# The end of a mixer kernel: last tile in three pieces, stores from ScalarE, no block around the program

## The chip, the cores and the metric

The kernel runs on one core of a Trainium2 chip. The time is the device time of one execution in microseconds (us), given as the median of several runs. Beside it stands a profiled execution, whose span runs from the first to the last instruction in the trace; an execution's time is somewhat longer than its span.

The engines of a core are TensorE (PE: matmuls; PEld: its weight loads), VectorE (DVE), ScalarE (ACT), GpSimd (POOL) and SyncE (SP, which here does nothing but issue transfers). Each runs its own list of instructions, and they wait for each other through semaphores. A transfer (DMA) is issued by an engine, moved by 16 DMA engines, and raises a semaphore when it has landed.

## The reference

```python
def reference(x, w1, w2, w3, w4):          # x: 1 x 2048 x 512, bf16
    B, S, D = x.shape
    h = _gelu(_layernorm(x, axis=-1) @ w1)             # w1: 512 x 512
    c = D // 4
    g0 = jnp.pad(h[:, :, 0*c:1*c], ((0, 0), (1, 0), (0, 0)))[:, :S, :]
    g1 = jnp.pad(h[:, :, 1*c:2*c], ((0, 0), (0, 1), (0, 0)))[:, 1:, :]
    g2 = jnp.pad(h[:, :, 2*c:3*c], ((0, 0), (2, 0), (0, 0)))[:, :S, :]
    g3 = jnp.pad(h[:, :, 3*c:   ], ((0, 0), (0, 2), (0, 0)))[:, 2:, :]
    hs = jnp.concatenate([g0, g1, g2, g3], axis=-1) @ w2   # w2: 512 x 512
    x1 = x + hs
    h2 = _gelu(_layernorm(x1, axis=-1) @ w3) @ w4      # w3: 512 x 1792, w4: 1792 x 512
    return x1 + h2
```

For the change only the last line matters: each output row is x1 plus a product with w4 that sums over 1792 = 14 x 128 hidden values.

## The kernel before

The 2048 rows are 16 tiles of 128. Each tile passes through a layer norm, a transpose, the product with w1 and a gelu ("up1"), the product with w2 on rows shifted by one or two ("mix"), a second layer norm and transpose, the product with w3 and a gelu ("up2"), and the product with w4 ("down"). A list, `SCRIPT`, gives the order of these steps for TensorE. A planner (`Program.order`) goes through all operations, with estimated durations and due times, and writes down one order per engine. `emit` then walks the plan and writes each operation into its engine's program, ahead of it the waits on semaphores that it needs (L635).

The names that the change touches:

- `mm_down` makes the down step of one tile: 14 matmuls (L511) into one bank of `o_ps`, a PSUM tensor with two banks that are used in turn; then a residual addition on VectorE (L519) from PSUM and x1 into `o_sb`; then a store of `o_sb` to the output (L522), issued by SP. A matmul that reuses a bank waits for the addition that last read it.
- `TAIL` gives the column pieces of the last tile (`last`, tile 15). All other tiles are done in one piece of 512 columns. With (256, 256) the last tile has two chains of 14 matmuls, two additions of 256 columns and two stores of 64 KB, each with rows of 512 bytes.
- `emit` opens a block (`with nc.Block() as block:`, L593). Each engine's instructions stand in a body of that block, which the engine branches into at the start. At the end of the block each engine drains, and a barrier over all five engines is passed: GpSimd gathers their arrivals and releases them. These instructions carry L593.
- After all operations SP waits for the semaphores of all 17 stores in turn (L655).

The last steps of TensorE are down 10, down 14 and down 15. ScalarE's last work is the gelu of the last up2 group, which is done about 101 us into the run. ScalarE issues one transfer in the whole kernel: half of the first tile of x (L292), whose other half SP issues.

Of the kernel before, what the change touches and what calls it, by code (L numbers as in the profile page):

```python
# [12 lines left out]
ENGINES = ["sp", "act", "pe", "dve", "pool"]  # L13
# [178 lines left out]
SQRT = (0,)  # L192
STAT_ACT = (1, 3, 6, 16, 23)
HALF = (0,)
TAIL = (256, 256)
LOADS = """
x2 x1 x0 x4-5 w1b w1a x3 w2 x6-7 w3 x8-11 x12-15 w4b tp19 w4a
"""
# [6 lines left out]
def bass_standalone__mixer_s_mlp__prompt_kernel(nc, x, w1, w2, w3, w4, out):  # L205
    B, S, D = x.shape
# [13 lines left out]
    with ExitStack() as es:  # L220
# [31 lines left out]
        pg = Program()  # L252
# [6 lines left out]
        def next_bank():  # L259
            nbank[0] += 1  # L260
            return (nbank[0] - 1) % NOB, nbank[0]
# [236 lines left out]
        def mm_down(t):  # L498
            g = group_of[2, t]
            oi = t % NO  # L500
            last = t == NT - 1
            c0 = 0
            for hh, W in enumerate(TAIL if last else (D,)):
                b, v = next_bank()
                dst = o_ps[:, b, 0:W]
                cs = slice(c0, c0 + W)
                c0 += W

                def f(e, dst=dst, cs=cs):
                    for fc in range(FC):  # L510
                        ins = e.matmul(dst, h2T[:, fc, P * t : P * (t + 1)], w4_sb[:, fc, cs],  # L511
                                       start=(fc == 0), stop=(fc == FC - 1))
                    return ins

                pg.add("pe", f"down{t}_{hh}", f,
                       reads=[(("w4", c), 0) for c in range(FC)] + [(("h2", j, g), 0) for j in range(FC)],
                       writes=[(("o", b), v)], dur=FC * (W * 0.4167 + 2.5))
                pg.add("dve", f"res{t}_{hh}",
                       (lambda d, c: (lambda e: e.tensor_tensor(o_sb[:, oi, c], d, x1_sb[:, t, c], ALU.add)))(dst, cs),  # L519
                       reads=[(("o", b), v), (("x1", t), 0)], writes=[(("osb", oi, hh), t)], dur=70 + W * 1.04)  # L520
                pg.add("sp", f"out_dma{t}_{hh}",
                       (lambda c: (lambda e: e.dma_start(outt[:, t, c], o_sb[:, oi, c])))(cs),  # L522
                       reads=[(("osb", oi, hh), t)], dur=400 * W / D, queue="sp")


        consts()
# [15 lines left out]
        if SQRT:  # L542
            pg.add("act", "warm_sqrt", lambda e: e.activation(warm[:], eps_c[:], ACT_F.Sqrt),
                   reads=[(("eps",), 0)], writes=[(("warm",), 0)], dur=1400)
        pg.add("act", "warm_gelu", lambda e: e.activation(warm[:], eps_c[:], ACT_F.Gelu_apprx_tanh),
               reads=[(("eps",), 0)] + [(("sdv", q), 0) for q in SQRT], writes=[(("warm",), 1)], dur=1400)
        steps = []
        for step in SCRIPT.split():
            kind, n = step.split(":")
            a, _, b = n.partition("-")  # L550
            steps += [(kind, n) for n in (range(int(a), int(b or a) + 1) if kind != "warm" else [int(n)])]
        pe_tp = {n for kind, n in steps if kind in ("tp", "ty")}
        queue = []
# [11 lines left out]
        for kind, n in steps:  # L565
            if kind == "warm":
                warm_pe(n)
            elif kind in ("tp", "ty"):
                pe_transpose(n % NT, n, kind == "ty")
            elif kind == "mix":  # L570
                mm_mix(n)
            elif kind == "down":
                mm_down(n)
            else:
                for _ in mm_up(int(kind[2]), n):
                    pass
        pg.line(queue)
        pg.order()
        emit(nc, es, pg)

def emit(nc, es, prog):

    engs = {"sp": nc.sync, "act": nc.scalar, "pe": nc.tensor, "dve": nc.vector, "pool": nc.gpsimd}
    sems = {e: es.enter_context(nc.semaphore("sem_" + e)) for e in ENGINES}
    ndma = 0
    for op in prog.seq:
        if op.queue is not None:
            op.stream = ("dma", ndma)
            sems[op.stream] = es.enter_context(nc.semaphore(f"sem_dma{ndma}"))
            ndma += 1  # L590
        else:
            op.stream = op.eng
    with nc.Block() as block:  # L593
        bodies = {}

        def keep(name):
            def _body(e):
                bodies[name] = nc.cur_body

            return _body  # L600

        block.gpsimd(keep("pool"))
        block.sync(keep("sp"))
        block.scalar(keep("act"))
        block.vector(keep("dve"))
        block.tensor(keep("pe"))
        know = {e: {} for e in ENGINES}
        implied = {}
        count = {}
        last_write, readers = {}, {}  # L610
        for op in prog.seq:
            e = op.eng
            needs = {}

            def need(sv):
                if needs.get(sv[0], 0) < sv[1]:
                    needs[sv[0]] = sv[1]

            for res, ver in op.reads:
                lw = last_write[res]  # L620
                assert lw[2] == ver, (op.name, res, ver, lw)
                need(lw)
            for res, ver in op.writes:
                if res in last_write:
                    need(last_write[res])
                for sv in readers.get(res, ()):
                    need(sv)
            if e == "pe":
                needs.pop("pe", None)
            k = know[e]  # L630
            with nc.body(bodies[e]):
                for s, v in sorted(needs.items(), key=lambda sv: -sv[1]):
                    if k.get(s, 0) >= v:
                        continue
                    engs[e].wait_ge(sems[s], v)  # L635
                    for s2, v2 in implied[(s, v)].items():
                        if v2 > k.get(s2, 0):
                            k[s2] = v2
                    k[s] = max(k.get(s, 0), v)
                ins = op.fn(engs[e])  # L640
                inc = 1 if op.queue is None else 16
                ins.then_inc(sems[op.stream], inc)
            val = count[op.stream] = count.get(op.stream, 0) + inc
            snap = dict(k)
            snap[op.stream] = max(snap.get(op.stream, 0), val)
            implied[(op.stream, val)] = snap
            for res, ver in op.reads:
                readers.setdefault(res, []).append((op.stream, val))
            for res, ver in op.writes:
                last_write[res] = (op.stream, val, ver)  # L650
                readers[res] = []
        with nc.body(bodies["sp"]):
            for op in prog.seq:
                if op.name.startswith("out_dma"):
                    nc.sync.wait_ge(sems[op.stream], 16)  # L655


# [26 lines left out]
```

## Time and profile before

| | us |
|---|---|
| median of 12 runs | 138.71 (138.18 to 139.49) |
| the profiled execution's time | 138.38 |
| its span | 136.6 |
| TensorE busy | 131.7 (96%) |
| VectorE, ScalarE, GpSimd busy | 58.8, 51.4, 19.4 |
| granted TensorE clock | 1.00 |

How to read it: a line of the profile names a group of instructions by the line of the kernel, the engine, the operation and the tiles written and read (out<-in), with counts, total and mean durations. "SPq" and "ACTq" are the sequencers of those engines, where transfers are issued. The chain of waits follows the work that ended last back to what released it; "issue" is time in which an engine waited for nothing that the profile shows. The timeline gives start and length in us from the start of the span; in brackets stands the idle time before an instruction and what ended it.

### The profile page before, as it was taken

The page shows a single profiled execution, that of the slowest core. Times are in us where ns is not written, and L with a number is a line of the kernel's source. Part 1 is how long each engine was busy: PE and PEld are TensorE (multiplying, and loading weights), DVE is VectorE, ACT ScalarE, POOL GpSimd, SP SyncE. Part 2 cuts the span into 40 slices and gives each one's busy share as a digit, 9 for nine tenths or more (in the row PEclk, how much of TensorE's full clock was granted, in tenths as well). Part 3 has the DMA queues.
Part 4 walks back from the last instruction along what each step waited for, and adds up shares of the span by engine and source line. Part 5 has one row for each costly group of instructions (what it writes and reads, how often), then busy time and mean ns, then how long its engine had stood idle before and what let it go on. Part 6 is the DMA issues. An engine that isn't in the chain of part 4 may idle for free.

```text
span 136.6 us, 1976 instructions
## 1 busy us (share of the span) xinstructions
PE 131.7 (96%) x773; PEld 73.3 (54%) x786; DVE 58.8 (43%) x169; ACT 51.4 (38%) x70; POOL 19.4 (14%) x43
## 2 busy tenths in 40 slices
PE   6989999999999999999999999999999999999992
PEld 2277878776668644444444444444444444444471
DVE  1797999998899640043610053210002222322231
ACT  4799657443667455530055520025550000000000
POOL 2342383332043410001010010000000000000000
DMA  4899966474269551001210003110001111111111
GB/s 107 288 347 403 364 224 118 94 100 79 59 211 187 100 103 38 0 0 38 82 38 0 0 0 76 40 38 5 0 0 34 43 38 38 43 38 38 51 64 41
DMA packets 21257, 12.19 MB, mean 89 GB/s; under 512 B 13568, under 2 KB 20736, under 8 KB 21248
## 3 DMA queue, kind: packets, MB, share of 16 engines
q1 hardware_dynamic: 21104, 12.00, 33.0%
q8 instruction: 6, 0.10, 0.3%
q10 hardware_dynamic: 144, 0.07, 0.2%
q14 instruction: 3, 0.02, 0.1%
HBM read 6.82 MB, written 2.10 MB: 65 GB/s over the span
## 4 chain that ended last, share of the span: by engine, by line
PE 85%; DVE 5%; POOL 3%; DMA 2%; issue 1%; SPq 1%; ACT 0%
PE y_ps L442 40%; PE o_ps L511 35%; PE o_ps L482 9%; POOL rstd L366 3%; DMA x_sb<-in_x_dram 2%; DVE xn_buf L372 1%; DVE st L349 1%; PE y_ps L415 1%; DVE x_sb L493 1%; POOL xn_buf L383 1%; SPq L296 1%; DVE x_sb L489 1%; DVE st6b L343 0%; DVE o_sb L519 0%; DVE vpe L355 0%
## 5 line engine op out<-in xcount | busy, mean ns | idle before, releaser
L442 PE MATMUL y_ps<-xnT,w_sb 128*128 128x256 bf16 (+2 forms) x435 | 64.1, 305 | 0.3
L442 PEld LDWEIGHTS y_ps<-xnT,w_sb 128*128 128x128 bf16 x440 | 40.4, 98 | 23.7 <-issue 0.2
L511 PE MATMUL o_ps<-w_sb,h2T 128*128 128x512 bf16 (+1 forms) x236 | 48.8, 366 | 0.1
L457 ACT ACTIVATE h2T<-y_ps 128x1024 bf16<-128x1024 f32 (+1 forms) x29 | 28.6, 994 | 36.6 <-PE y_ps L442 36.5
L511 PEld LDWEIGHTS o_ps<-w_sb,h2T 128*128 128x128 bf16 x238 | 23.3, 98 | 25.3
L519 DVE TENSOR_TENSOR o_sb<-o_ps,x_sb 128x512 bf16<-128x512 f32 (+1 forms) x17 | 11.2, 660 | 44.6 <-PE o_ps L511 44.3
L366 POOL TENSOR_TENSOR rstd<-vpe,neghalf 128x1 f32<-128x1 f32 x31 | 16.9, 558 | 61.8 <-DVE vpe L355 53.4
L493 DVE TENSOR_TENSOR x_sb<-o_ps,x_sb 128x512 bf16<-128x512 f32 x14 | 9.6, 689 | 22.2 <-PE o_ps L482 22.2
L349 DVE BATCH_NORM_STATS2 st<-x_sb 128x6 f32<-128x512 bf16 x26 | 17.5, 684 | 2.2 <-DMA x_sb<-in_x_dram 2.1
L482 PE MATMUL o_ps<-w_sb,hT 128*128 128x512 bf16 x58 | 15.0, 379 | 0.3
L372 DVE TENSOR_SCALAR xn_buf<-x_sb,mv,rstd 128x512 bf16<-128x512 bf16 x25 | 10.2, 411 | 3.8 <-POOL rstd L366 2.8
L457 ACT ACTIVATE hT<-y_ps 128x1024 bf16<-128x1024 f32 (+1 forms) x10 | 8.5, 852 | 7.7 <-PE y_ps L442 7.6
L482 PEld LDWEIGHTS o_ps<-w_sb,hT 128*128 128x128 bf16 x64 | 6.1, 98 | 5.3
L535 PE MATMUL o_ps<-zeros 128*128 128x512 bf16 x12 | 5.2, 627 | 1.2 <-DVE zeros L269 1.2
L380 ACT ACTIVATE xn_buf<-x_sb,nmr,rstd 128x512 bf16<-128x512 bf16 x5 | 4.0, 810 | 2.6 <-DVE nmr L376 2.6
L351 DVE BATCH_NORM_AGGREGATE mv<-st 128x2 f32<-128x6 f32 x26 | 4.1, 173 | 0.2
L535 PEld LDWEIGHTS o_ps<-zeros 128*128 128x128 bf16 x12 | 1.7, 145 | 3.9 <-issue 2.7
L355 DVE TENSOR_SCALAR vpe<-mv 128x1 f32<-128x1 f32 x26 | 3.5, 148 | 0.3
L324 ACT ACTIVATE junk<-x_sb 128x512 bf16<-128x512 bf16 x5 | 3.1, 628 | 0.7 <-DVE x_sb L489 0.7
L415 PEld LDWEIGHTS y_ps<-ident,xn_buf 128*128 128x128 bf16 x28 | 1.8, 98 | 1.8 <-DVE xn_buf L372 1.3
L415 PE MATMUL y_ps<-ident,xn_buf 128*128 128x128 bf16 x28 | 2.4, 220 | 0.3 <-DVE xn_buf L372 0.2
L420 ACT ACTIVATE xnT<-y_ps 128x512 bf16<-128x512 bf16 (+1 forms) x5 | 2.6, 548 | 0.1
(33 smaller groups left out, 18.9 us busy)
## 6 DMA issues: line engine op xcount, KB each, us to landing
out_dram<-o_sb SPq DMA_DIRECT2D x15, 128.0 KB, 1.7
w_sb<-in_w_dram SPq DMA_DIRECT2D x1, 1792.0 KB, 10.0
w_sb<-in_w_dram SPq DMA_DIRECT2D x2, 896.0 KB, 9.6
x_sb<-in_x_dram SPq DMA_DIRECT2D x2, 512.0 KB, 12.0
x_sb<-in_x_dram SPq DMA_DIRECT2D x2, 256.0 KB, 4.7
w_sb<-in_w_dram SPq DMA_DIRECT2D x2, 256.0 KB, 3.7
w_sb<-in_w_dram SPq DMA_DIRECT2D x1, 512.0 KB, 5.8
x_sb<-in_x_dram SPq DMA_DIRECT2D x3, 128.0 KB, 2.4
```

The source lines that it names most:

```text
L349: pg.add("dve", f"bnst{q}", lambda e: e.bn_stats(st6[:, q, :], src), reads=rs, writes=[(("st6", q), 0)], dur=605)
L351: pg.add("dve", f"bnag{q}", lambda e: e.bn_aggr(mv[:, q, :], st6[:, q, :]), reads=[(("st6", q), 0)], writes=[(("mv", q), 0)], dur=75)
L366: lambda e: e.tensor_tensor(col(rstd), col(vpe), neghalf[:], ALU.pow),
L372: lambda e: e.tensor_scalar(dst, src, mv[:, q, 0:1], rstd[:, q : q + 1], ALU.subtract, ALU.mult),
L415: ins = e.transpose(chunk(c), xn_buf[:, slot(q), P * c : P * (c + 1)], ident[:])
L442: ins = e.matmul(y_ps[:, p, W * i : W * (i + 1)], wsb[:, dc, P * fc : P * (fc + 1)], src[:, dc, P * t0 : P * t0 + W], start=(dc == 0), sto ...
L457: (lambda d, s: (lambda e: e.activation(d, s, ACT_F.Gelu_apprx_tanh)))(dst, ysrc),
L482: ins = e.matmul(dst, hT[:, j, c0 : c0 + P], w2_sb[:, j, :], start=(j == 0), stop=(j == DC - 1))
L493: f = lambda e: e.tensor_tensor(x1_sb[:, t, :], dst, x_sb[:, t, :], ALU.add)
L511: ins = e.matmul(dst, h2T[:, fc, P * t : P * (t + 1)], w4_sb[:, fc, cs], start=(fc == 0), stop=(fc == FC - 1))
L519: (lambda d, c: (lambda e: e.tensor_tensor(o_sb[:, oi, c], d, x1_sb[:, t, c], ALU.add)))(dst, cs),
L535: ins = e.matmul(o_ps[:, b, :], zeros[:, 0:P], zeros[:], start=True, stop=True)
```

## The change

The last tile is made in three pieces of 256, 128 and 128 columns. Its three stores are issued by ScalarE and no longer by SP; the last two are of 32 KB, with rows of 256 bytes. `emit` writes all instructions straight into the program, with no block: the branch into the block, the branch out of it, the drains and the closing barrier are gone. SP still waits for all stores (now 18) at the end. The plan of everything else is the same: on every engine the other instructions stand in the same order with the same waits.

```diff
-TAIL = (256, 256)
+TAIL = (256, 128, 128)
...
-                pg.add("sp", f"out_dma{t}_{hh}",
+                pg.add("act" if last else "sp", f"out_dma{t}_{hh}",
                        (lambda c: (lambda e: e.dma_start(outt[:, t, c], o_sb[:, oi, c])))(cs),
-                       reads=[(("osb", oi, hh), t)], dur=400 * W / D, queue="sp")
+                       reads=[(("osb", oi, hh), t)], dur=400 * W / D, queue="act" if last else "sp")
...
-    with nc.Block() as block:
-        bodies = {}
-
-        def keep(name):
-            def _body(e):
-                bodies[name] = nc.cur_body
-
-            return _body
-
-        block.gpsimd(keep("pool"))
-        block.sync(keep("sp"))
-        block.scalar(keep("act"))
-        block.vector(keep("dve"))
-        block.tensor(keep("pe"))
...
-            with nc.body(bodies[e]):
-                for s, v in sorted(needs.items(), key=lambda sv: -sv[1]):
...
-                ins = op.fn(engs[e])
-                inc = 1 if op.queue is None else 16
-                ins.then_inc(sems[op.stream], inc)
+        for s, v in sorted(needs.items(), key=lambda sv: -sv[1]):
...
+        ins = op.fn(engs[e])
+        inc = 1 if op.queue is None else 16
+        ins.then_inc(sems[op.stream], inc)
...
-        with nc.body(bodies["sp"]):
-            for op in prog.seq:
-                if op.name.startswith("out_dma"):
-                    nc.sync.wait_ge(sems[op.stream], 16)
+    for op in prog.seq:
+        if op.name.startswith("out_dma"):
+            nc.sync.wait_ge(sems[op.stream], 16)
```

The rest of the diff is the same code with one level of indentation less.

More of the change, by code (lines that the diff above doesn't have):

```diff
@@ L592, in emit @@
             op.stream = op.eng
-    with nc.Block() as block:
-        bodies = {}
-        def keep(name):
-            def _body(e):
-                bodies[name] = nc.cur_body
-            return _body
-        block.gpsimd(keep("pool"))
-        block.sync(keep("sp"))
-        block.scalar(keep("act"))
-        block.vector(keep("dve"))
-        block.tensor(keep("pe"))
[L607 to L610, printed above, removed]
-        for op in prog.seq:
[L612 to L630, printed above, removed]
-            with nc.body(bodies[e]):
-                for s, v in sorted(needs.items(), key=lambda sv: -sv[1]):
[L633 to L639, printed above, removed]
-                ins = op.fn(engs[e])
-                inc = 1 if op.queue is None else 16
-                ins.then_inc(sems[op.stream], inc)
[L643 to L651, printed above, removed]
-        with nc.body(bodies["sp"]):
-            for op in prog.seq:
-                if op.name.startswith("out_dma"):
-                    nc.sync.wait_ge(sems[op.stream], 16)
@@ new lines, in emit, with need @@
+    know = {e: {} for e in ENGINES}
+    implied = {}
+    count = {}
+    last_write, readers = {}, {}
+    for op in prog.seq:
+        e = op.eng
+        needs = {}
+        def need(sv):
+            if needs.get(sv[0], 0) < sv[1]:
+                needs[sv[0]] = sv[1]
+        for res, ver in op.reads:
+            lw = last_write[res]
+            assert lw[2] == ver, (op.name, res, ver, lw)
+            need(lw)
+        for res, ver in op.writes:
+            if res in last_write:
+                need(last_write[res])
+            for sv in readers.get(res, ()):
+                need(sv)
+        if e == "pe":
+            needs.pop("pe", None)
+        k = know[e]
+        for s, v in sorted(needs.items(), key=lambda sv: -sv[1]):
+            if k.get(s, 0) >= v:
+                continue
+            engs[e].wait_ge(sems[s], v)
+            for s2, v2 in implied[(s, v)].items():
+                if v2 > k.get(s2, 0):
+                    k[s2] = v2
+            k[s] = max(k.get(s, 0), v)
+        ins = op.fn(engs[e])
+        inc = 1 if op.queue is None else 16
+        ins.then_inc(sems[op.stream], inc)
+        val = count[op.stream] = count.get(op.stream, 0) + inc
+        snap = dict(k)
+        snap[op.stream] = max(snap.get(op.stream, 0), val)
+        implied[(op.stream, val)] = snap
+        for res, ver in op.reads:
+            readers.setdefault(res, []).append((op.stream, val))
+        for res, ver in op.writes:
+            last_write[res] = (op.stream, val, ver)
+            readers[res] = []
@@ L659 @@
+    for op in prog.seq:
+        if op.name.startswith("out_dma"):
+            nc.sync.wait_ge(sems[op.stream], 16)
 _INS = ['x', 'w1', 'w2', 'w3', 'w4']
```

## The prediction, made before the result was known

> **What bounds the kernel now.** I read the page's busy times first, then the chain of waits at the two ends of the run, then the timeline of the last microseconds, and last the DMA table and the records of the closing barrier.
>
> The busy line shows which engine sets the pace:
>
> ```profile
> PE 131.7 (96%) x773; PEld 73.3 (54%) x786; DVE 58.8 (43%) x169; ACT 51.4 (38%) x70; POOL 19.4 (14%) x43
> ```
>
> TensorE is busy for 96% of the 136.6 us span, and the other engines for less than half of it. The chain of waits, from 100 us on, says that nothing but matmuls stands on the path until the last one is done:
>
> ```profile
> 99.99 0.81 PE y_ps L442 x3
> 100.80 9.93 PE o_ps L511 x46
> ...
> 121.58 12.52 PE o_ps L511 x71
> 134.09 0.02 issue
> 134.11 0.42 DVE o_sb L519
> ```
>
> So the time is made of a head (before TensorE has work), a body that this change doesn't touch, and a tail of 136.6 - 134.1 = 2.5 us after the last matmul. The change touches one branch in the head, the last 1.5 us of matmuls, and the tail. The timeline of the tail (start, length):
>
> ```profile
> 131.11 0.69 DVE L519 TENSOR_TENSOR o_sb<-o_ps,x_sb 128x512 bf16<-128x512 f32 x1 [2.39 <-PE o_ps L511]
> 132.59 0.42 DVE L519 TENSOR_TENSOR o_sb<-o_ps,x_sb 128x256 bf16<-128x256 f32 x1 [0.78 <-PE o_ps L511]
> 134.11 0.42 DVE L519 TENSOR_TENSOR o_sb<-o_ps,x_sb 128x256 bf16<-128x256 f32 x1 [1.10 <-PE o_ps L511]
> ...
> 134.57 0.33 SPq L522 DMA_DIRECT2D out_dram<-o_sb  x1
> ```
>
> The second residual addition ends at 134.11 + 0.42 = 134.53; SP issues the last store at 134.57. The records of SP's final waits (L655) and of the closing block (L593), asked for the stretches in which they fall, give the rest:
>
> ```profile
> L655 SPq EVENT_SEMAPHORE  x1: 28/28/28, 136.1 to 136.1; - x1
> L593 SPq COMPARE_BRANCH  x1: 33/33/33, 136.2 to 136.2; - x1
> L593 SPq DRAIN  x1: 7/7/7, 136.3 to 136.3; - x1
> L593 POOLq EVENT_SEMAPHORE  x2: 17/17/17, 136.4 to 136.5; - x2
> L593 PEldq EVENT_SEMAPHORE  x1: 51/51/51, 136.5 to 136.5; - x1
> ```
>
> The last wait starts in the stretch 136.10 to 136.15, so it is done by about 136.15. Then SP branches, drains, tells GpSimd, which gathers and releases all five engines; TensorE's release ends the span at 136.6. The tail is therefore 0.44 residual addition and hop, 1.54 from the store's issue to its landing, about 0.03 wait record, and 0.45 closing barrier.
>
> **The change part by part.**
>
> *The closing barrier goes.* In the changed kernel SP's last instruction is the last of its waits for the stores. Removed: branch, drain, gather, release, 136.15 to 136.6. All of it stood on the path, since nothing runs beside it: -0.45 us. Bounds: -0.40 (the records' rounding) to what lies outside the span. The profiled execution took 138.38 us with a span of 136.6, so 1.78 us are not in the span. If the four other engines now end their own programs up to 30 us before SP does, some of that 1.78 may leave the path too; I take nothing for it and keep a case for it. The Trainium skill (Runtime: NRT & Kernel Launch, "The ~15µs preamble/postamble breakdown") says that the runtime puts its own barrier of about 1.5 us behind a kernel to wait for all engines. By that rule the kernel's barrier is a second one, and its removal loses no order; it could speak against the change only if the runtime's barrier grew by what ours shrank, and then the sum would be without the 0.45. The trace ends before it. I take the row, because SP, the last to arrive, arrives 0.45 earlier.
>
> *The branch at the start goes.* The chain of waits has 0.07 us of issue ahead of SP's first load, against 0.06 and 0.05 ahead of the next ones:
>
> ```profile
> 0.65 0.07 issue
> 0.72 0.40 SPq L296
> 1.12 0.06 issue
> 1.18 0.42 SPq L296
> 1.60 0.05 issue
> ```
>
> A branch costs between 0 and 0.07 here; the one branch with a record took 33 ns. I take -0.03. The first loads stand on the chain, so the whole run moves by it.
>
> *The last tile in three pieces.* In place of 14 matmuls of 256 columns there are 28 of 128, all on the path. Their pitch is read from the head, where the same shapes occur in a row:
>
> ```profile
> 8.17 2.73 PE y_ps L442 x48
> ...
> 18.11 6.11 PE y_ps L442 x56
> 24.23 0.05 issue
> ...
> 25.09 3.49 PE y_ps L442 x32
> ```
>
> The 48 are of 128 columns: 2.73 / 48 = 57 ns. The 56 and the 32 are of 256 columns: 109 ns each, and the two residual additions of the last tile, 134.11 - 132.59 = 1.52 us apart, agree (14 x 109 = 1.53). So 28 x 57 = 1.59 against 1.53: +0.06 us (0 to +0.07).
>
> The third piece gets the first piece's PSUM bank back (two banks in turn), so its first matmul waits for the first piece's residual addition. That ends at 132.59 + 0.42 = 133.01; VectorE to TensorE took 0.06 where the head shows it (normalization ending at 6.56, transpose at 6.62): 133.07. The second piece keeps TensorE busy until about 132.57 + 14 x 0.057 = 133.37. The wait is hidden with 0.3 us to spare. What is queued behind it is only the third piece itself; TensorE's sequencer had handed out its whole program at 132.0, when its final drain began (that drain lasted 2155 ns), so it feeds faster than the array eats. Without that cover the stall would be the addition and the hop, 0.48.
>
> Behind the last matmul stands a residual addition of 128 columns. The rows by form give 692 ns for 512 and 424 for 256:
>
> ```profile
> L519 DVE TENSOR_TENSOR o_sb<-o_ps,x_sb 128x512 bf16<-128x512 f32 x15 | 10.4, 692 | 42.7 <-PE o_ps L511 42.4
> L519 DVE TENSOR_TENSOR o_sb<-o_ps,x_sb 128x256 bf16<-128x256 f32 x2 | 0.8, 424 | 1.9 <-PE o_ps L511 1.9
> ```
>
> That is 268 / 256 = 1.05 ns a column, so 424 - 134 = 290 ns: -0.13 us. The additions of the other two pieces end before the next piece is multiplied and hide under it.
>
> *The last three stores move to ScalarE.* It has been idle since 101.9 us (its drain began at 100.8 and took 1.05), so nothing is queued in front of them; they are issued at about 133.05, 133.70 and 134.5, further apart than the 0.3 to 0.4 one issue takes. They leave SP's queue, where only the final waits follow; nobody is served sooner or later by that. VectorE to ScalarE took 0.02 in the head (mv at 5.60 to sdv at 5.62), VectorE to SP 0.04 here; the half loads of x took 0.39 to issue on ScalarE and 0.42 on SP. I take 0 for the change of issuer.
>
> The landing is the unknown. The DMA table:
>
> ```profile
> out_dram<-o_sb SPq DMA_DIRECT2D x15, 128.0 KB, 1.7
> out_dram<-o_sb SPq DMA_DIRECT2D x2, 64.0 KB, 1.5
> x_sb<-in_x_dram ACTq DMA_DIRECT2D x1, 64.0 KB, 2.6
> x_sb<-in_x_dram SPq DMA_DIRECT2D x1, 64.0 KB, 3.1
> ```
>
> Halving a store took 0.2 off. The last store of 64 KB moved its bytes only in 135.3 to 135.8 (the DMA share of those stretches), 0.45 of its 1.54 us; the rest is issue, start and receipt. With 32 KB there are as many rows (128), each of 256 bytes. From the row: 1.4 to 1.55, and I take 1.49, or -0.05. The rule that speaks against the change is in the skill's DMA: Bandwidth & Descriptors, "Specifications": at least 512 bytes are needed for full rate, and below that the engine reads, modifies and writes. No store of before has such rows. If it doubled the 0.45 us of moving bytes the landing would be 2.0: +0.45 in place of -0.05. I stay near the row, as most of the landing is not bytes.
>
> *Sum.* -0.45 - 0.03 + 0.06 - 0.13 + 0 - 0.05 = -0.60 us. Against the profiled execution: a span of 136.0 and 137.8 us. That execution was 0.33 below the median of 138.71, which I take as the spread of runs; so 138.1 us for the median, -0.43%. With the skill's rule for small rows: -0.10, 138.6. A change under 0.3% (0.42 us) can hardly be told from none in runs that spread from 138.18 to 139.49.
>
> **The rivals.**
>
> 1. *Likeliest: the sum holds*, within 0.2 of -0.60: 138.1 us, 137.85 to 138.4. For it: nearly all of it is a barrier and an addition whose records are at the end of the path.
>
> 2. *The small store gives it back.* Rows of 256 bytes write slowly, or the runtime's end takes over the barrier's time: -0.10 to -0.3, 138.5 us, no change. For it: no row of before. Against it: the landing hardly follows the bytes.
>
> 3. *More than the span is saved.* The other engines end early, and up to half a microsecond of the 1.78 us outside the span goes with the barrier: -1.0, 137.7 us. For it: four of five engines have nothing to do after the last addition. Against it: SP still has to end, and may be the slowest to.
>
> 4. *Slower: the store issued by ScalarE lands late.* Its only DMA of before landed after 2.6 us. If that were its price for a store too, against 1.49, the end would be 1.1 later and the sum +0.5: 139.2 us. It decides from a landing of about 2.5 us (0.60 + 0.42 above 1.49). Against it: SP's twin of that load took 3.1, at a time when the DMA engines were busy, so the 2.6 is the load of the head and not ScalarE.
>
> **How the numbers follow.** Chances: 0.56 for the sum, 0.20 for the second, 0.14 for the third, 0.10 for the slower case. The sum's lower edge is near the bound of 0.42, so about 0.08 of its chance belongs to no change: faster 0.56 - 0.08 + 0.14 = 0.62, same 0.20 + 0.08 = 0.28, slower 0.10. The range takes in the second and third cases and leaves out the slower one: 137.4 to 138.8.
>
> **What the changed profile would show.** Right: the span ends within 0.05 of SP's last wait, with no drain and no release behind it; the last addition takes 0.29; the third piece starts without a gap, 28 matmuls in 1.6 us; ScalarE's last store lands after 1.4 to 1.55; span near 136.0, with still 1.8 outside it. Wrong: a landing of 2 us or more, an idle TensorE ahead of the third piece, or a distance from span to time that has changed by as much as the barrier took.

## The result, and the profile after

The changed kernel takes 137.50 us (median of 12 runs, 137.03 to 140.25), the kernel before 138.52 (49 runs in all, 137.97 to 140.24). The ratio is 0.9916, with a 95% interval of 0.9893 to 0.9939: faster, as forecast, but by about twice the forecast 0.43%. Executions in a slower state are left out of the ratio; of the 12 that is the one of 140.25, and the other 11 have a median of 137.35. The time lies in the predicted range (137.4 to 138.8), near its lower end.

The profiled execution of the changed kernel took 137.19 us. Its last record ends at 135.87; in the execution before, which took 138.38, the last record ended at 136.57. So the span fell by 0.70, and what lies between span and time fell too, from 1.81 to 1.32. The forecast had the first and took nothing for the second. (From the rounded span of 136.6 it had 1.78 in place of 1.81.)

The chain of waits of the changed kernel, from 121 us on (start, length, what):

```profile
121.45 12.55 PE o_ps L511 x85
134.00 0.02 issue
134.02 0.29 DVE o_sb L519
```

It has the links of before, and the last one is shorter: 0.29 in place of 0.42. The timeline of its last microseconds:

```profile
130.98 0.69 DVE L519 TENSOR_TENSOR o_sb<-o_ps,x_sb 128x512 bf16<-128x512 f32 x1 [2.39 <-PE o_ps L511]
...
132.46 0.42 DVE L519 TENSOR_TENSOR o_sb<-o_ps,x_sb 128x256 bf16<-128x256 f32 x1 [0.78 <-PE o_ps L511]
132.91 1.77 ACTq L522 DMA_DIRECT2D out_dram<-o_sb  x3
133.24 0.29 DVE L519 TENSOR_TENSOR o_sb<-o_ps,x_sb 128x128 bf16<-128x128 f32 x1 [0.36 <-PE o_ps L511]
134.02 0.29 DVE L519 TENSOR_TENSOR o_sb<-o_ps,x_sb 128x128 bf16<-128x128 f32 x1 [0.49 <-PE o_ps L511]
```

The three additions of the last tile start 0.78 us apart, about what 14 matmuls of 128 columns take (14 x 0.057 = 0.80); there is no gap ahead of the third piece. ScalarE issues the last store at 132.91 + 1.77 - 0.34 = 134.34 (one issue takes 0.34). The last of SP's final waits (L639 here) begins between 135.80 and 135.85:

```profile
L639 SPq EVENT_SEMAPHORE  x1: 28/28/28, 135.8 to 135.8; - x1
```

Nothing follows it: the span ends with it, at 135.87. Set side by side, the profiled executions give, in us:

| piece of the end | before | after |
|---|---|---|
| start of the last full tile's addition to start of the last addition | 3.00 | 3.04 |
| last addition | 0.42 | 0.29 |
| from its end to the store's issue | 0.04 | 0.03 |
| issue to landing | 1.54 | 1.49 |
| from the landing to the end of the span (last wait; before, the closing barrier too) | 0.46 | 0.04 |
| span to time | 1.81 | 1.32 |
| sum | 7.27 | 6.21 |

That is 1.06 us. The rest of the difference of these two executions, 138.38 - 137.19 = 1.19, is 0.13 in the head, where a half of the first tile of x landed after 2.98 in place of 3.10. That load scatters between executions of any kernel here (2.91 in the control run below), so it is not a gain of the change.

### The profile page after: what moved, and what is told of

Read it like the earlier page. It is cut to its first block, busy times and chain, and to the rows that moved or that the text cites. A ratio compares the mean times of both kernels' runs of the same rounds, so it can differ in the third digit from the quotient of the medians.

```text
span 135.9 us, 1995 instructions
## 1 busy us (share of the span) xinstructions
PE 130.8 (96%) x787; PEld 73.4 (54%) x800; DVE 59.0 (43%) x170; ACT 51.4 (38%) x70; POOL 19.4 (14%) x43
## 4 chain that ended last, share of the span: by engine, by line
PE 85%; DVE 5%; POOL 3%; DMA 2%; issue 1%; SPq 1%; ACT 0%
PE y_ps L442 40%; PE o_ps L511 36%; PE o_ps L482 9%; POOL rstd L366 3%; DMA x_sb<-in_x_dram 2%; DVE xn_buf L372 1%; DVE st L349 1%; PE y_ps L415 1%; DVE x_sb L493 1%; POOL xn_buf L383 1%; SPq L296 1%; DVE x_sb L489 1%; DVE st6b L343 0%; DVE vpe L355 0%; DVE mv L351 0%
## 5 line engine op out<-in xcount | busy, mean ns | idle before, releaser
L511 PE MATMUL o_ps<-w_sb,h2T 128*128 128x512 bf16 (+2 forms) x250 | 48.8, 355 | 0.1
L519 DVE TENSOR_TENSOR o_sb<-o_ps,x_sb 128x512 bf16<-128x512 f32 (+2 forms) x18 | 11.4, 633 | 44.3 <-PE o_ps L511 44.1
L535 PE MATMUL o_ps<-zeros 128*128 128x512 bf16 x12 | 4.4, 540 | 1.2 <-DVE zeros L269 1.2
```

The lines of the kernel that those rows point to most:

```text
L535: ins = e.matmul(o_ps[:, b, :], zeros[:, 0:P], zeros[:], start=True, stop=True)
```

## The experiments

In all of them the distance between span and time is looked at beside the time. The spans of one kernel scatter by more than a microsecond from execution to execution, while the distance of one kernel stays within about 0.1. Part of the scatter can be read in the kept traces: half a tile of x lands after 2.89 to 3.27 us, and in three of them (the control run, the block alone, the two unequal pieces) TensorE waits 0.5 to 0.6 us for a transfer that transposes a tile, near 29.7 us, where neither execution of the section above waits. In the control run:

```profile
PE y_ps L442 <- DMA xnT<-xn_buf: 0.6, 1, 0.6
```

So half a microsecond that would need many runs to be seen in the times is plain in the distance. Distances are medians over the executions of a kernel. Shown spans are rounded to 0.1, so one distance is known to 0.05; for the profiled executions the end of the span is given to 0.01, from the last record.

My theory after the result was the third rival of the prediction: with the barrier gone, four engines end their programs before SP does, and part of what follows a program's end outside the span leaves the path. Rivals: chance; the stores issued by ScalarE; the branch out of the block, if instructions had to be fetched behind it.

**The kernel before, again.**

> The kernel before, unchanged, as a control for the distance between span and time. All theories: the distance is 1.73 to 1.83 us in every execution, as in the profiled one (138.38 - 136.6 = 1.78); with the block it does not vary. If it varies from 1.3 to 1.8, the half microsecond that the changed kernel gained outside the span is chance and not the block.

Measured: ratio to the other runs of before 1.0018 (0.9987 to 1.0049), distance 1.81 (1.78 to 1.87 in ten executions); in the 33 executions of before beside them 1.81 as well. The distance belongs to the kernel and is not chance.

**The block alone.**

```diff
 # the changed kernel with
-TAIL = (256, 128, 128)
+TAIL = (256, 256)
-                pg.add("act" if last else "sp", f"out_dma{t}_{hh}",
+                pg.add("sp", f"out_dma{t}_{hh}",
```

(and `queue="sp"` for all stores.)

> Only the block goes; the last tile stays in two pieces of 256 columns, stored by SP. My theory: the closing barrier takes 0.45 of the span and the other engines' early end takes 0.45 to 0.5 outside it: span about 136.1, distance 1.33, about 0.93 us less than before (ratio 0.993). Rival (the stores from ScalarE end the program sooner outside the span): distance 1.78 here, and only 0.45 less (ratio 0.9968).

Measured: 137.59 us, ratio 0.9914 (0.9885 to 0.9943), distance 1.32. From the start of the last addition (134.61) to the end of the span (136.65) it takes 2.04, against 136.57 - 134.11 = 2.46 before: 0.42 less, the closing barrier. The span is 136.6 and not the expected 136.1, because this execution is one of those with TensorE's wait of 0.5 for the transposing transfer. Block and barrier by themselves carry the whole gain that the times can show.

**The pieces and ScalarE's stores alone.**

```diff
 # the kernel before with
-TAIL = (256, 256)
+TAIL = (256, 128, 128)
-                pg.add("sp", f"out_dma{t}_{hh}",
+                pg.add("act" if last else "sp", f"out_dma{t}_{hh}",
```

(and `queue="act"` for the last tile's stores.)

> Only the three pieces and the stores from ScalarE; the block and its closing barrier stay. My theory: +0.06 matmuls, -0.13 addition, -0.05 landing, so 0.1 to 0.2 us less in the span, distance 1.78 as before: ratio 0.9985 to 0.9992. Rival (ScalarE's stores account for the gain outside the span): distance 1.33, ratio 0.995.

Measured: 138.21 us, ratio 0.9966 (0.9935 to 0.9997), distance 1.83. So the stores from ScalarE do nothing for the distance, and that rival falls. The last addition to the end takes 136.46 - 134.19 = 2.27, against 2.46 before, while the tile's matmuls take 0.03 more (134.19 - 131.16 = 3.03 against 3.00). The trace gives this part about 0.16, within the 0.1 to 0.2 expected. The median time says more (0.34%, or 0.5 us), but its interval reaches to 0.9997.

**A barrier without a block.**

```diff
     for op in prog.seq:
         if op.name.startswith("out_dma"):
             nc.sync.wait_ge(sems[op.stream], 16)
+    nc.all_engine_barrier()
```

> The changed kernel with a barrier over all five engines put behind SP's waits, but still with no block, so no branches. My theory (what was saved outside the span is that the four other engines end early): they now end together with SP again, so the span grows by 0.4 to 0.45 and the distance goes back to 1.78: about 138.0, 0.9 above the changed kernel. Rival (the branch out of the block, behind which the code has to be fetched): the distance stays 1.33 and only the span grows, 0.45 above the changed kernel.

Measured: 138.00 us, ratio 0.9942 (0.9909 to 0.9976), distance 1.83. The last wait begins at 136.1 and the barrier's records (L640) follow it:

```profile
L640 SPq DRAIN  x1: 7/7/7, 136.2 to 136.2; - x1
L640 SPq EVENT_SEMAPHORE  x1: 17/17/17, 136.3 to 136.3; - x1
...
L640 PEldq EVENT_SEMAPHORE  x1: 51/51/51, 136.4 to 136.4; - x1
```

With no branch and no block at all the distance is back at 1.8. The branch, and any fetch behind it, falls as a cause; holding all engines back is enough. The span's share is smaller than I wrote: 136.41 - 134.30 = 2.11 from the last addition, against 135.87 - 134.02 = 1.85 in the changed kernel, so about 0.26 and not 0.4 to 0.45. The rest of the 0.42 of a block's end is its branch: from the end of SP's last wait to the start of its drain it takes 0.20 in the kernel before (136.15 to 136.35) and 0.04 here (136.157 to 136.194), while drain and barrier behind it take 0.22 in both. The 33 ns of the branch's record are a small part of these 0.16.

**Which engine's end is it?** In each of the next runs the changed kernel got one more wait for the last store, on one more engine:

```diff
+    last = [op for op in prog.seq if op.name.startswith("out_dma")][-1]
+    nc.tensor.wait_ge(sems[last.stream], 16)      # or nc.gpsimd, nc.vector
```

> The changed kernel, where TensorE too waits for the last store before it ends; SP waits as before, the three other engines still end early. Theory A (each engine has an end of its own outside the span, and a slower one than SP's sets the time as soon as that engine is late): if TensorE is the slow one, the distance between span and time goes from 1.33 to about 1.8; otherwise it stays 1.33 to 1.4. Theory B (the ends of five engines at once hold each other up): one engine more costs a part, 1.4 to 1.5, whichever engine it is. The span grows by 0.05 at most in both.

> As the run before, with GpSimd in place of TensorE waiting for the last store. Theory A: 1.8 if GpSimd is the slow one, else 1.33 to 1.4. Theory B: 1.4 to 1.5.

> As the run before, with VectorE waiting for the last store. Theory A: 1.8 if VectorE is the slow one, else 1.33 to 1.4. Theory B: 1.4 to 1.5.

And in one run ScalarE does the final waits and SP none:

```diff
-            nc.sync.wait_ge(sems[op.stream], 16)
+            nc.scalar.wait_ge(sems[op.stream], 16)
```

> The changed kernel, where ScalarE does all the final waits for stores in place of SP; SP ends about 4 us early. Theory A: the distance becomes ScalarE's own end, 1.8 if it is the slow one, below 1.33 if its end is shorter than SP's. Theory B: one engine is late, as in the changed kernel, so 1.33. The span stays within 0.1, since a wait that is over takes about 0.03 on SP.

Measured:

| last to end | distance, median (range) | ratio to before |
|---|---|---|
| SP (the changed kernel) | 1.34 (1.28 to 1.38) | 0.9916 (0.9893 to 0.9939) |
| SP and VectorE | 1.45 (1.42 to 1.48) | 0.9954 (0.9921 to 0.9988) |
| ScalarE, no SP | 1.48 (1.43 to 1.53) | 0.9952 (0.9919 to 0.9986) |
| SP and TensorE | 1.57 (1.56 to 1.59, 3 runs) | 0.9920 (0.9881 to 0.9959) |
| SP and GpSimd | 1.87 (1.83 to 1.91) | 0.9970 (0.9949 to 0.9992) |

GpSimd is the slow one. In its run the wait's record is this (its line, engine, duration and start):

```profile
L641 POOLq EVENT_SEMAPHORE  x1: 17/17/17, 135.9 to 135.9; - x1
```

GpSimd thus ends with SP, at the end of the span (135.95). From the last addition (134.10) the span takes 1.85 as in the changed kernel, and the profiled execution took 137.81, against 137.19; 0.08 of that lies ahead of the last addition. One wait of 17 ns on an engine that had been idle for 50 us costs half a microsecond, none of it inside the span.

The single distances fit neither theory as I wrote it: Theory A had every engine but one at 1.33 to 1.4, where VectorE, ScalarE and TensorE have 1.45 to 1.57, and Theory B had 1.4 to 1.5 for all, where TensorE and GpSimd lie above. What A becomes with these numbers is that each engine has an end of its own and the longest one counts. One run tells this from a sum of the parts, which would be 1.84: all engines but GpSimd late.

```diff
+    last = [op for op in prog.seq if op.name.startswith("out_dma")][-1]
+    for e in (nc.tensor, nc.vector, nc.scalar):
+        e.wait_ge(sems[last.stream], 16)
```

> The changed kernel, where TensorE, VectorE and ScalarE wait for the last store like SP, and GpSimd alone ends early. Theory A (the time outside the span is the largest of the late engines' own ends: SP 1.33, VectorE 1.45, ScalarE 1.48, TensorE 1.57, GpSimd 1.87): 1.57, as with TensorE alone. Theory B (ends at once hold each other up): the parts add, (0.24 + 0.12 + 0.15) above 1.33, so 1.8.

Measured: distance 1.60 (1.55 to 1.65), ratio 0.9944 (0.9904 to 0.9984). It is TensorE's end and not the sum. All three waits are on record at the end of the span:

```profile
L642 ACTq EVENT_SEMAPHORE  x1: 17/17/17, 135.9 to 135.9; - x1
L642 DVEq EVENT_SEMAPHORE  x1: 21/21/21, 135.9 to 135.9; - x1
L642 PEldq EVENT_SEMAPHORE  x1: 51/51/51, 135.9 to 135.9; - x1
```

So the 1.81 of before is GpSimd's end, to within a few hundredths: before, GpSimd's last record ends at 136.48, 0.09 ahead of the span's end, so 1.81 + 0.09 = 1.90 follow it, against 1.87 when it alone is held with SP. The next longest end, TensorE's 1.57, does not reach so far. What each engine does in its end no trace here shows; that is left open.

**Who issues the last stores.** The changed kernel with `out_dma` on SP for all tiles:

```diff
-                pg.add("act" if last else "sp", f"out_dma{t}_{hh}",
+                pg.add("sp", f"out_dma{t}_{hh}",
```

> The changed kernel, with the last three stores issued by SP in place of ScalarE. My theory: the issuer is worth nothing; from the last addition's start to the end of the span 1.80 to 1.90, as with ScalarE (135.87 - 134.02 = 1.85), distance 1.33. Rival (a cold instruction or queue makes one of them slower): 0.1 or more between them.

Measured: 137.27 us (4 runs), ratio 0.9925 (0.9900 to 0.9949), distance 1.37. The last addition starts at 134.07 and the span ends at 135.92, so 1.84 against 1.85. In the profile's table of DMA issues the small stores of this kernel read

```profile
out_dram<-o_sb SPq DMA_DIRECT2D x1, 64.0 KB, 1.5
out_dram<-o_sb SPq DMA_DIRECT2D x2, 32.0 KB, 1.5
```

and in the changed kernel

```profile
out_dram<-o_sb ACTq DMA_DIRECT2D x1, 64.0 KB, 1.5
out_dram<-o_sb ACTq DMA_DIRECT2D x2, 32.0 KB, 1.5
```

The issuer makes no difference that can be seen, and that step of the change is worth nothing here.

**Two pieces of unequal width.**

```diff
-TAIL = (256, 128, 128)
+TAIL = (384, 128)
```

> The changed kernel with pieces of 384 and 128 columns. My theory: 384 columns take 14 x 0.16, 128 take 14 x 0.057, so 3.04 for the tile against 3.12 with three pieces; the addition of 384 (about 0.56) hides under the second piece; behind the last matmul the same 1.85. So 0 to 0.08 less than the changed kernel: 137.3 to 137.5, within what can be told of the changed kernel. Rival (the second piece waits for the addition of the tile before, or the large store of 96 KB delays the last one): 0.1 or more behind the changed kernel's 1.85.

Measured: 137.78 us, ratio 0.9940 (0.9912 to 0.9968), distance 1.31. In the trace the last full tile's addition starts at 131.57 and the last one at 134.57: 3.00, so the 0.04 that the three pieces had added is gone. From there to the end of the span it is 136.43 - 134.57 = 1.86, as in the changed kernel (1.85). So the trace agrees with the estimate, but the times don't: 137.78 is above the expected 137.3 to 137.5. The profiled execution has TensorE's wait of 0.5 for the transposing transfer, and spans scatter by far more than 0.04. No version better than the changed kernel is shown.

## Why the prediction was right in direction and too small

**The sum inside the span held.** Forecast -0.60, measured -0.57 (the table's first five rows). Some of that closeness is small misses that cancel. Term by term:

- Closing barrier: -0.45 forecast, -0.42 measured.
- Last addition: -0.13 forecast, -0.13 measured; the line through 512 and 256 columns gave 290 ns, and the profile has 292.
- Landing: -0.05 forecast, 1.49 taken, 1.49 measured, so the 2.0 that the forecast made of the Trainium skill's rule (DMA: Bandwidth & Descriptors, "Specifications") by doubling the time of the bytes is not there. In stretches of a tenth of a microsecond the changed kernel shows the bytes of the last store moving in 0.2 to 0.3 us (columns: stretch, its length, busy of PE, PEld, DVE, ACT, POOL, clock, DMA share, GB/s):

```profile
135.10:135.20 0.10, 0.00 (x0) 0.00 (x0) 0.00 (x0) 0.00 (x0) 0.00 (x0) 1.00 0.06 15
135.20:135.30 0.10, 0.00 (x0) 0.00 (x0) 0.00 (x0) 0.00 (x0) 0.00 (x0) 1.00 0.79 182
135.30:135.40 0.10, 0.00 (x0) 0.00 (x0) 0.00 (x0) 0.00 (x0) 0.00 (x0) 1.00 0.61 123
135.40:135.50 0.10, 0.00 (x0) 0.00 (x0) 0.00 (x0) 0.00 (x0) 0.00 (x0) 1.00 0.04 8
```

The 64 KB store of before moved its bytes in about 0.35 us (the forecast read 0.45 off coarser stretches). Over 135.1 to 135.8 us the packets of the last store took these shares of the 16 DMA engines' time, 64 KB before and 32 KB after:

```profile
q1 hardware_dynamic: 144, 0.07, 32.7%
q10 hardware_dynamic: 144, 0.03, 21.5%
```

Half the bytes took two thirds of the time. So rows of 256 bytes did cost about 1.3 times as much per byte, but in a landing of 1.49 us, most of which is not bytes, that does not show as a delay.

- Matmuls: +0.06 forecast, +0.04 measured. The third piece's wait for its PSUM bank stayed covered, as worked out.
- Issuer: 0 forecast, -0.01 measured from the addition's end to the store's issue, which is no more than rounding. (Before, addition and hop are 134.57 - 134.11 = 0.46, where the forecast's tail has 0.44; no term of the sum uses it.)
- Branch at the start: -0.03 forecast, nothing measured. SP's first load starts at 0.72 with and without the block:

```profile
0.66 0.07 issue
0.72 0.40 SPq L296
```

The 0.07 of issue ahead of it, which I had offered as an upper bound for the branch, is there without a branch too. Nor are the 33 ns of a record the cost of a branch: the one at the block's end took 0.16 of the barrier's 0.42.

**The step that failed** is the one on what lies outside the span: "some of that 1.78 may leave the path too; I take nothing for it and keep a case for it." It was worth 0.49 us in the profiled executions and 0.47 in the medians (1.81 to 1.34), about as much as the barrier itself. It is the sign that the forecast had named for being wrong, a distance that changes by as much as the barrier took. The mechanism of the third rival was right, and its size too (up to half a microsecond); it had been given a chance of 0.14. The objection I had put against it, that SP "may be the slowest to" end, was an open question that I answered in the wrong direction: SP's end is the shortest of the five, GpSimd's the longest. So the barrier had held the engine with the longest end until the last moment, and without it the shortest end counts. Forecast and missing term together are -1.07, against -1.06 in the two traces' ends, -1.02 in the medians (-1.17 with the 137.35) and about -1.16 by the ratio.

The skill's account of a runtime barrier behind the kernel (Runtime: NRT & Kernel Launch, "The ~15µs preamble/postamble breakdown") led me to ask only whether that barrier would take back what the kernel's saved. It did not; no run shows that barrier itself, since the traces end before it. What the runs show is the other side: behind each engine's program follows a stretch of its own length, 1.34 to 1.87 us here, and an engine held back by a barrier starts it late.

**The rivals.** A slow small store, and a store from ScalarE that lands after 2.5 us, are refuted by the 1.49. So ScalarE as the issuer does not explain the 2.6 of its load of x; that the head's traffic does is likely but not shown.

## What to carry to other kernels

A barrier over all engines at the end cost twice here: what the trace shows of it, and outside the span the longest of the engines' ends, which then begin together, in place of the shortest. Let only one engine wait for the last stores, the one whose end is shortest (here SP), and let the others run out; GpSimd above all should not be held. When a change touches the end of a program, subtract the span from the time in every execution: here that distance was steady to about 0.1 us where the times scatter by more than one.

## What the runs showed that was not expected

- From the end of the span to the end of the measured time it is 1.34 us if SP alone ends last, 1.45 with VectorE, 1.48 for ScalarE, 1.57 with TensorE and 1.87 with GpSimd; of several late ones the longest counts (1.60 with all but GpSimd).
- A bare barrier over all engines added about 0.26 to the span, the end of a block 0.42; the difference is the block's branch, whose record shows only 0.03.
- A store of 32 KB in rows of 256 bytes landed after 1.49 us, one of 64 KB in rows of 512 bytes after 1.54; per byte the small rows took about 1.3 times as long.
